# Attention and soft mixture-of-experts in one fp32 kernel: transposes in half-row pairs, one ring of four PSUM bank pairs, and one written-out order

## The chip, the cores and the metric

The kernel runs on one core of a Trainium2 chip. Its engines are TensorE (PE in the profile, with its weight loads shown apart as PEld), VectorE (DVE), ScalarE (ACT), GpSimd (POOL) and SyncE (SP), whose queue issues the DMAs. The metric is the device time of one execution in microseconds.

## The reference

Eight batches of eight heads attend over 576 positions of 64 values. The attention output, one row per token, goes through a soft mixture of experts: every token is spread over 32 slots (8 experts of 4), each expert is a two-layer network, and the slots are mixed back. All is fp32.

```python
scores = scale * q @ k.T + bias            # 576 x 576 per head; bias: a small MLP of positions
attn = exp(scores - max) / (sum + 1e-9)
x = (attn @ v)                             # heads side by side: 4608 tokens x 512
logits = x @ phi                           # 4608 x 32
d = softmax of logits over the tokens;  slot_input = d.T @ x
slot_out[e] = relu(slot_input[e] @ w1[e]) @ w2[e]
out = softmax of logits over the slots @ slot_out
```

## The kernel before

First the position bias of all heads is made (`bias_group`, 36 groups) and written to DRAM. Then come 32 units, `units`: four head pairs `hp`, each over eight batches. A unit has five row tiles p of queries. Row tiles 0 to 3 hold 128 queries of each of the two heads; row tile 4 holds the last 64 queries of both heads.

For each row tile, `score` (L257) multiplies queries with keys. The two heads stand in the lower and upper 64 rows of the PE array (L279), so the PE runs them as two 64x128 tiles; row tile 4 uses the whole array with a weight matrix that is half zeros (L270). DVE adds the bias and takes the extreme (L247), ACT takes the exponential and the sum (L250), DVE inverts the sum (L285, L286), and POOL scales the rows (L255). `turn` (L296) transposes the result 128x128 at a time (L309, L313, L317, L321), 41 blocks a unit, into single PSUM banks, which ACT or DVE copies to the tile `at` (`Split.copy`, L53 and L59, picks the engine by a running account). `mix` (L325) multiplies `at` with `v`: four parts with the two heads side by side in 64 columns each (L337), and a rest on the whole array (L340). The result `xt` goes to DRAM (`xs`) for the first three head pairs.

In the last head pair (units 24 to 31) `moe` (L346) does the token work of a batch beside the attention: it fetches the other heads' part back (`xo`, L353), transposes the tokens (L364, L370; 20 blocks), multiplies with `phi` (logits, L377), gathers running extremes and sums (L387, L389), transposes the powers (L431, L432) and sums into the slots (L463, L466). After unit 31 the experts' two layers run (L646, L673), with their weights `wt` streamed in, and the output is mixed and written (L702, L708).

Three PSUM pools hold the eight banks: `ps_s` two pairs, `ps_t` three single banks, `ps_o` one. The order of the attention comes from a loop over n = 5u + p: transposes run two row tiles behind the scores, and `mix` and the token steps are put in at offsets (`MIXL`, `MOEO`). The framework's scheduler then orders the instructions by its own estimate.

Of the kernel before, what the change touches and what calls it, by code (L numbers as in the profile page):

```python
# [19 lines left out]
W1N = 21  # L20
# [5 lines left out]
JB = (0, 0, 0, 0, 0)  # L26
MOEO = (1, 2, 2, 3, 3, 4, 5, 6, 6)
FEO = 0
FW = {(24, 2): 1, (31, 0): 1, (31, 1): 1, (31, 2): 1, (31, 3): 1, (31, 4): 1, (31, 8): 2, (31, 9): 3, 162: 1, 163: 1, 164: 3}
MIXE = (0.2, 0.2)  # L30
MOE1 = (1, 1, 2, 2, 2, 3, 5.3, 5.3, 5.8, 4, 5.8)
MOE2 = (0.7, 0.7, 0.7, 0.5, 0.7, 0.6, 0.9, 0.9, 0.95)
MIXL = ((2, 3), (1, 2))
# [31 lines left out]
def body(ctx, tc, qk, v, wcol, phi, mw1, mw2, tabh, consth, out):  # L65
# [23 lines left out]
    ld = Split(nc)  # L89

# [38 lines left out]
    def ready():  # L129

        nc.sync.dma_start(out=phis, in_=phi.rearrange("(g p) s -> p g s", p=P))
        with tc.issue_after(last["dve"].ins):
            nc.vector.tensor_scalar(out=phis, in0=phis, scalar1=-1.0, scalar2=None, op0=ALU.mult)
            nc.vector.tensor_add(out=rsum[:, 0:32], in0=ident[:, 0:32], in1=ident[:, 32:64])
            nc.vector.tensor_add(out=rsum[:, 0:32], in0=rsum[:, 0:32], in1=ident[:, 64:96])
            nc.vector.tensor_add(out=rsum[:, 0:32], in0=rsum[:, 0:32], in1=ident[:, 96:128])
            for r in range(1, 4):
                nc.vector.tensor_copy(out=rsum[:, 32 * r:32 * r + 32], in_=rsum[:, 0:32])
        with tc.issue_after(last["pool"].ins):
            for t in (lp, et, et2):  # L140
                nc.gpsimd.memset(t, 0.0)
# [11 lines left out]
    pc = ps_t.tile([P, 512], F32, name="pc", tag="t")  # L153
# [35 lines left out]
    def bias_group():  # L189
# [7 lines left out]
        pb = ps_s.tile([P, 2, 512], F32, name="pb", tag="s")  # L197
# [21 lines left out]
    def load_qk(u):  # L219


        hp, b = units[u]
        x = st[u]["qk"] = ldp.tile([P, 1280], F32, name="qk", tag="qk")
        nc.sync.dma_start(out=x, in_=qk[b, hp])
# [21 lines left out]
    def soft(ps, bias, y, mn, sm):  # L246
        last["dve"] = nc.vector.tensor_tensor_reduce(  # L247
            out=y.rearrange("a (x n) -> a x n", x=2), in0=ps[:, :, 0:HALF], in1=bias.rearrange("a (x n) -> a x n", x=2),
            scale=-QS, scalar=3.0e38, op0=ALU.add, op1=ALU.min, accum_out=mn)
        nc.scalar.activation(out=y, in_=y, func=AF.Exp, bias=mn, scale=-1.0, accum_out=sm)  # L250
        ld.a(851)
        ld.d(S)

    def norm(out, y, r):
        last["pool"] = nc.gpsimd.tensor_scalar(out=out, in0=y, scalar1=r, scalar2=1.0, op0=ALU.mult, op1=ALU.mult)  # L255

    def score(u, p):  # L257


        d = st[u]  # L260
        hp, b = units[u]
        x = d["qk"]
        y = d["y", p] = yp.tile([P, 2 * S], F32, name="y", tag="y")
        mn = smp.tile([P, 2], F32, name="mn", tag="mn")
        sm = smp.tile([P, 2], F32, name="sm", tag="sm")
        bias = biases[hp][p]
        if p == 4:
            ps = ps_s.tile([P, 2, 512], F32, name="ps", tag="s")
            for n in range(2):
                nc.tensor.matmul(ps[:, n, 0:HALF], x[:, 1152:1280], x[:, 64 + n * HALF:64 + (n + 1) * HALF], start=True,  # L270
                                 stop=True)
            soft(ps, bias, y[:, 0:S], mn[:, 0:1], sm[:, 0:1])
        else:
            pss = [ps_s.tile([P, 2, 512], F32, name="ps", tag="s") for _ in range(2)]
            for n in range(2):
                for hh in range(2):
                    rs = slice(64 * hh, 64 * hh + 64)
                    k0 = 64 * (1 - hh) + n * HALF
                    nc.tensor.matmul(pss[hh][:, n, 0:HALF], x[rs, 640 + p * P:640 + (p + 1) * P], x[rs, k0:k0 + HALF],  # L279
                                     start=True, stop=True, tile_position=(64 * hh, 0))  # L280
            for hh in range(2):
                hs = slice(S * hh, S * hh + S)
                soft(pss[hh], bias[:, hs], y[:, hs], mn[:, hh:hh + 1], sm[:, hh:hh + 1])
        r = sm[:, 0:1] if p == 4 else sm
        nc.vector.tensor_scalar(out=r, in0=r, scalar1=1e-9, scalar2=None, op0=ALU.add)  # L285
        nc.vector.reciprocal(out=r, in_=r)  # L286
        ld.d(0)
        ld.d(0)
        if p == 4:
            norm(y[:, S:S + 64], y[:, 512:576], r)  # L290
            norm(y[:, 0:S], y[:, 0:S], r)
        else:
            for g in range(2):
                norm(y[:, S * g:S * g + S], y[:, S * g:S * g + S], sm[:, g:g + 1])

    def turn(u, p, j):  # L296

        d = st[u]
        ch, cc = (p // 2, p % 2) if p < 4 else (1, 2)
        if p in (0, 2) and j == 0:  # L300
            d["at", ch] = atp.tile([P, 9, 256 + 64 * ch], F32, name="at", tag=f"at{ch}")
        at = d["at", ch]
        y = d["y", p]
        pt = ps_t.tile([P, 512], F32, name="pt", tag="t")
        if p < 4:
            if j < 2:
                for kk in range(4):
                    k0 = 640 * j + kk * P
                    nc.tensor.transpose(out=pt[:, kk * P:(kk + 1) * P], in_=y[:, k0:k0 + P], identity=ident)  # L309
                ld.copy(at[:, 4 * j:4 * j + 4, cc * P:(cc + 1) * P], pt.rearrange("a (x n) -> a x n", x=4), 512)  # L310
            else:
                for i in range(2):
                    nc.tensor.transpose(out=pt[:, i * P:(i + 1) * P], in_=d["y", p - 1 + i][:, 512:640], identity=ident)  # L313
                ld.copy(at[:, 8, 0:256], pt[:, 0:256], 256)
        elif j == 0:
            for kk in range(4):
                nc.tensor.transpose(out=pt[:, kk * P:(kk + 1) * P], in_=y[:, kk * P:(kk + 1) * P], identity=ident)  # L317
            ld.copy(at[:, 0:8, 256:320].rearrange("a (h k) n -> a k h n", h=2),
                    pt.rearrange("a (k h n) -> a k h n", k=4, h=2), 512)
        else:  # L320
            nc.tensor.transpose(out=pt[:, 0:P], in_=y[:, 512:640], identity=ident)  # L321
            ld.copy(at[0:64, 8, 256:320], pt[0:64, 0:64], 64)
            ld.copy(at[64:128, 8, 256:320], pt[64:128, 64:128], 64)

    def mix(u, ch, j):  # L325

        d = st[u]
        at, w = d["at", ch], 256 if ch == 0 else 320
        if j == 0:
            d["po", ch] = ps_o.tile([P, 512], F32, name="po", tag="o")  # L330
            if ch == 0:
                d["xt"] = xts[:, u % 2, :]
        po, xt = d["po", ch], d["xt"]
        for kk in (2 * j, 2 * j + 1):
            for hh in range(2):
                v0 = 64 * (4 * hh + kk)
                nc.tensor.matmul(po[64 * hh:64 * hh + 64, 0:w], d["v"][:, v0:v0 + 64], at[:, 4 * hh + kk, 0:w],  # L337
                                 start=kk == 0, stop=False, tile_position=(0, 64 * hh))
        if j == 1:
            nc.tensor.matmul(po[:, 0:w], d["v"][:, 512:640], at[:, 8, 0:w], start=False, stop=True)  # L340
            ld.copy(xt[:, 256 * ch:256 * ch + w], po[:, 0:w], w)
            hp, b = units[u]
            if ch == 1 and hp < NP - 1:
                nc.sync.dma_start(out=xs[b, hp], in_=xt)

    def moe(u):  # L346

        hp, b = units[u]
        m = {}

        def fetch():
            m["xo"] = xp.tile([P, NP - 1, S], F32, name="xo", tag="xo")
            nc.sync.dma_start(out=m["xo"], in_=xs[b].rearrange("g p j -> p g j"))  # L353

# [3 lines left out]
        def tokens(g):  # L358
            if g == 0:
                m["xk"] = xp.tile([P, 5, DM], F32, name="xk", tag="xk")  # L360
            gs = slice(g * P, (g + 1) * P)
            px = ps_t.tile([P, 512], F32, name="px", tag="t")
            for c in range(4):
                nc.tensor.transpose(out=px[:, c * P:(c + 1) * P], in_=X(g)[:, c * P:(c + 1) * P], identity=ident)  # L364
# [16 lines left out]
        def dispatch():  # L381
# [12 lines left out]
            for i, cs in parts:  # L394
                nc.vector.tensor_reduce(out=mb[:, i:i + 1], in_=pr[:, cs], axis=AX.X, op=ALU.min)
# [374 lines left out]
```

## Time and profile before

| | |
|---|---|
| time, median of 3 runs | 741.37 us (740.66 to 743.53) |
| the profiled execution's own time | 743.72 us |
| its span | 741.9 us |
| granted TensorE clock, mean | 0.989 |
| PE / DVE / ACT / POOL busy | 713.3 / 505.7 / 440.6 / 279.7 us |
| DMA moved | 111.52 MB |

The page gives busy time by engine, the span in 40 slices, the DMA queues and the costliest groups of instructions. A matmul's recorded duration includes its way through the array, so matmuls that follow each other overlap in the records: how fast the PE works is read from the distance between starts. In a timeline row the columns are start, duration of the merged group, engine, line, operation, tiles, shape and count. An fp32 matmul is two instructions, a transpose one.

### The profile page before, as it was taken

The numbers are of one execution on the slowest core, as the hardware profiler recorded it, in microseconds if no ns is written. First come the engines' busy times: TensorE is split into PE (matmuls) and PEld (weight loads), VectorE is DVE, ScalarE is ACT, GpSimd is POOL, SyncE is SP. The second block draws the span as 40 slices with busy tenths as digits, with TensorE's granted clock in tenths as the row PEclk, the third lists the DMA queues.
The fourth block names the chain that finished last, engine by engine and source line by source line (L and its number), as shares of the span: only waits on it lengthen the run. The fifth ranks groups of instructions, "written<-read, shape, count | busy, mean of one in ns | idle before, by whom it ended". The sixth has DMA issues, their size and how long they took to land. (4 is left out here: it accounts for less than half of the span.)

```text
span 741.9 us, 14863 instructions
## 1 busy us (share of the span) xinstructions
PE 713.3 (96%) x5295; PEld 434.8 (59%) x5295; DVE 505.7 (68%) x1416; ACT 440.6 (59%) x1043; POOL 279.7 (38%) x355
## 2 busy tenths in 40 slices
PE   6999999999999999999999999999999999989973
PEld 3334566666666666666666666665566556553542
DVE  8998876676676777677676677666767676552333
ACT  5776656666666666666666666656555556532233
POOL 7993544443444434434444444333222322200000
PEclk9999999999999999999999999999999999999997
DMA  6567992332622223372322237230233024476999
GB/s 226 198 207 248 341 356 93 103 93 87 210 71 70 70 73 103 99 213 75 118 70 70 77 102 220 90 98 22 86 101 101 23 81 144 168 257 204 351 362 331
DMA packets 54680, 111.52 MB, mean 150 GB/s; under 512 B 7120, under 2 KB 24784, under 8 KB 54608
## 3 DMA queue, kind: packets, MB, share of 16 engines
q1 hardware_dynamic: 54608, 110.59, 45.6%
q8 instruction: 42, 0.69, 0.4%
q14 instruction: 30, 0.25, 0.1%
HBM read 83.44 MB, written 27.13 MB: 149 GB/s over the span
## 5 line engine op out<-in xcount | busy, mean ns | idle before, releaser
L255 POOL TENSOR_SCALAR y<-y,sm 128x576 f32<-128x576 f32 (+1 forms) x320 | 221.6, 703 | 357.3 <-DVE sm L286 107.4
L250 ACT ACTIVATE y<-y,mn 128x576 f32<-128x576 f32 x288 | 221.5, 770 | 179.0 <-DVE mn L247 177.6
L247 DVE CUSTOM_DVE_ANT_0 y<-ps,bm 128x576 f32<-128x576 f32 x256 | 184.2, 758 | 49.9 <-PE ps L279 41.4
L279 PE MATMUL ps<-qk 64*128 64x288 f32 x1024 | 172.6, 430 | 0.6 <-DVE mn L247 0.5
L337 PE MATMUL po<-at,v 128*64 128x320 f32 (+1 forms) x1024 | 152.2, 418 | 1.1 <-ACT at L53 1.1
L309 PEld LDWEIGHTS pt<-ident,y 128*128 128x128 f32 x1024 | 114.4, 141 | 41.7 <-POOL y L255 22.7
L309 PE MATMUL pt<-ident,y 128*128 128x128 f32 x1024 | 137.9, 277 | 0.3 <-ACT at L53 0.3
L59 DVE COPY at<-pt 128x512 f32<-128x512 f32 (+2 forms) x188 | 107.5, 577 | 36.8 <-PE pt L309 26.6
L53 ACT COPY at<-pt 128x512 f32<-128x512 f32 (+2 forms) x228 | 107.1, 486 | 33.9 <-PE pt L309 30.3
L279 PEld LDWEIGHTS ps<-qk 64*128 64x128 f32 x1024 | 98.0, 186 | 35.3 <-issue 19.2
L337 PEld LDWEIGHTS po<-at,v 128*64 128x64 f32 x1024 | 62.2, 136 | 68.5 <-issue 29.6
L200 PE MATMUL pb<-f,wbd 128*32 128x64 f32 (+1 forms) x576 | 62.6, 421 | 2.2 <-DVE f L183 1.8
L183 DVE TENSOR_SCALAR f<-tabs,scl,nb 128x576 f32<-128x576 f32 x96 | 62.4, 727 | 0.6 <-DMA tabs<-in_tab_dram 0.6
L285 DVE TENSOR_SCALAR sm<-sm 128x2 f32<-128x2 f32 (+1 forms) x160 | 26.2, 163 | 53.3 <-ACT y L250 50.8
L183 POOL TENSOR_SCALAR f<-tabs,scl,nb 128x576 f32<-128x576 f32 x19 | 55.3, 2919 | 5.9 <-DMA tabs<-in_tab_dram 3.7
L250 ACT ACTIVATION_READ_ACCUMULATOR y<-y,mn 128x1 f32 x288 | 53.8, 187 | 0.0
L340 PE MATMUL po<-at,v 128*128 128x320 f32 (+1 forms) x128 | 48.1, 458 | 0.0
L200 PEld LDWEIGHTS pb<-f,wbd 128*32 128x32 f32 x576 | 24.1, 110 | 40.6 <-DVE f L183 20.6
L270 PE MATMUL ps<-qk 128*128 128x288 f32 x128 | 36.5, 407 | 0.0
L204 ACT ACTIVATE e<-pb,bcon 128x576 f32<-128x576 f32 x36 | 26.5, 737 | 15.7 <-PE pb L200 7.0
L340 PEld LDWEIGHTS po<-at,v 128*128 128x128 f32 x128 | 19.0, 188 | 28.0 <-issue 27.5
L247 DVE CUSTOM_DVE_ANT_0 y<-ps,br 128x576 f32<-128x576 f32 x32 | 24.2, 758 | 15.0 <-PE ps L270 14.5
(161 smaller groups left out, 560.6 us busy)
## 6 DMA issues: line engine op xcount, KB each, us to landing
wt<-in_moe_w_dram SPq DMA_DIRECT2D x64, 512.0 KB, 7.3
qk<-in_qk_dram SPq DMA_DIRECT2D x32, 640.0 KB, 5.1
v<-in_v_dram SPq DMA_DIRECT2D x32, 320.0 KB, 3.0
bias_m<-e SPq DMA_DIRECT2D x32, 288.0 KB, 2.3
out_dram<-ob SPq DMA_DIRECT2D x16, 512.0 KB, 5.2
xs<-xts SPq DMA_DIRECT2D x24, 288.0 KB, 2.9
xo<-xs SPq DMA_DIRECT2D x8, 864.0 KB, 6.6
bm<-bias_m SPq DMA_DIRECT2D x16, 288.0 KB, 2.9
```

What stands on the lines that cost most here:

```text
L53: nc.scalar.copy(out=out, in_=in_)
L59: nc.vector.tensor_copy(out=out, in_=in_)
L183: eng.tensor_scalar(out=f, in0=tabs[:, s0:s0 + S], scalar1=scl[:, sc:sc + 1], scalar2=nb1[:, 0:1], op0=ALU.mult, op1=ALU.max)
L200: nc.tensor.matmul(pb[32 * t:32 * t + 32, n, 0:w], wbd, fb[t][:, 512 * n:512 * n + w], start=True, stop=True, tile_position=(0, 32 * t))
L247: last["dve"] = nc.vector.tensor_tensor_reduce(out=y.rearrange("a (x n) -> a x n", x=2), in0=ps[:, :, 0:HALF], in1=bias.rearrange("a (x n) ...
L250: nc.scalar.activation(out=y, in_=y, func=AF.Exp, bias=mn, scale=-1.0, accum_out=sm)
L255: last["pool"] = nc.gpsimd.tensor_scalar(out=out, in0=y, scalar1=r, scalar2=1.0, op0=ALU.mult, op1=ALU.mult)
L270: nc.tensor.matmul(ps[:, n, 0:HALF], x[:, 1152:1280], x[:, 64 + n * HALF:64 + (n + 1) * HALF], start=True, stop=True)
L279: nc.tensor.matmul(pss[hh][:, n, 0:HALF], x[rs, 640 + p * P:640 + (p + 1) * P], x[rs, k0:k0 + HALF], start=True, stop=True, tile_position= ...
L309: nc.tensor.transpose(out=pt[:, kk * P:(kk + 1) * P], in_=y[:, k0:k0 + P], identity=ident)
L337: nc.tensor.matmul(po[64 * hh:64 * hh + 64, 0:w], d["v"][:, v0:v0 + 64], at[:, 4 * hh + kk, 0:w], start=kk == 0, stop=False, tile_position ...
L340: nc.tensor.matmul(po[:, 0:w], d["v"][:, 512:640], at[:, 8, 0:w], start=False, stop=True)
```

## The change

Half-row transposes: a 128x128 block is turned by two matmuls in transpose mode, one on the lower and one on the upper 64 rows, each with 64 moving columns of the identity and its own PSUM bank (`half_turn`). PSUM becomes four pairs of banks, handed round in order of release (`Banks`); scores, transposes, mixes and token steps all draw from it. Row tile 4's scores run as two 64x64 tiles without zeros, and the rest of `mix` as two 64-column tiles. Every step of attention and token work (S scores, t bias add, e exponential, m sum, n scale, T and R transposes, c copies, M mix, x copy of the mix, K, L, D, C, W, Z the token steps) gets a fixed place and, for copies, a fixed engine from a table, `PLAIN` for units 0 to 23 and `LAST` for 24 to 31; a place unit is a fifth of a unit. DMA loads are tied to steps of the table. The steps are issued in sorted order, and the framework's scheduler leaves them so.

```diff
+PLAIN = {
+    "lq": (-3.918, 0), "S0": (0.000, 0), "t0.0": (0.681, 0), "t0.1": (1.219, 0), "e0.0": (1.221, 0),
...
-    ps_s = ctx.enter_context(tc.tile_pool(name="ps_s", bufs=2, space=PSUM))
-    ps_t = ctx.enter_context(tc.tile_pool(name="ps_t", bufs=3, space=PSUM))
-    ps_o = ctx.enter_context(tc.tile_pool(name="ps_o", bufs=1, space=PSUM))
+    psp = ctx.enter_context(tc.tile_pool(name="psp", bufs=1, space=PSUM))
...
+    idle = [0, 1, 2, 3]
+
+    class Banks:
+        def __init__(self, n=1):
+            self.k, self.n = idle.pop(0), n
+            self.t = ps(self.k)
+
+        def read(self):
+            self.n -= 1
+            if self.n == 0:
+                idle.append(self.k)
+            return self.t
+
+    def then(u, name, f):
+        last = units[u][0] == NP - 1
+        place, eng = (LAST if last else PLAIN)[name]
+        prog.append((5 * u + place + (SHIFT if last else 0), len(prog), lambda: f(eng)))
...
+    def half_turn(out, src, r):
+        rs = slice(64 * r, 64 * r + 64)
+        nc.tensor.matmul(out, src[rs], ident[rs, rs], is_transpose=True, start=True, stop=True, tile_position=(64 * r, 0))
...
+                    if p == 4:
+                        nc.tensor.matmul(pss[0].t[rs, n, 0:HALF], x[rs, 1152:1216], x[rs, 64 + n * HALF:64 + (n + 1) * HALF],
+                                         start=True, stop=True, tile_position=(64 * hh, 64 * hh))
...
+        def turn(_):
+            pt = d["T", p] = Banks(2 if p < 4 else 3)
+            y = d["y", p]
+            for kk in range(8 if p < 4 else 5):
+                k0 = P * kk + 128 * (kk // 4) if p < 4 else P * kk
+                for r in range(2):
+                    half_turn(pt.t[:, r, 64 * kk:64 * kk + 64], y[:, k0:k0 + P], r)
+
+        step(u, f"T{p}", turn)
...
+                for hh in range(2):
+                    v0 = 64 * (4 * hh + i) if i < 4 else 512 + 64 * hh
+                    nc.tensor.matmul(po[64 * hh:64 * hh + 64, 0:w], d["v"][:, v0:v0 + 64],
+                                     d["at", c][:, 4 * hh + i if i < 4 else 8, 0:w], start=i == 0, stop=i == 4,
+                                     tile_position=(0, 64 * hh))
+
+            step(u, f"M{c}.{i}", part)
...
+        if u + 2 < U:
+            then(u, "S4", lambda _, u=u: load_qk(u + 2))
+            then(u, "M1.4", lambda _, u=u: load_v(u + 2))
+        if hp >= 1 and u - B < W1N:
+            then(u, "S1", lambda _: fetch_w(1))
...
+    with tc.manual_schedule():
+        for _, _, f in sorted(prog, key=lambda x: x[:2]):
+            f()
```

How the PE's rows stand in a unit of the first three head pairs. Before, two thirds of a unit (19 rows make a whole one): ps is a score, pt a transpose, po a mix.

```order
L279 MATMUL ps<-qk 128x288 x4
L337 MATMUL po<-at,v 64x320 x4
L309 MATMUL pt<-ident,y 128x128 x8
L279 MATMUL ps<-qk 128x288 x4
L337 MATMUL po<-at,v 64x320 x4
L340 MATMUL po<-at,v 128x320
L309 MATMUL pt<-ident,y 128x128 x8
L313 MATMUL pt<-ident,y 128x128 x2
L270 MATMUL ps<-qk 128x288 x2
L309 MATMUL pt<-ident,y 128x128 x8
L279 MATMUL ps<-qk 128x288 x4
L337 MATMUL po<-at,v 64x256 x4
```

Now, a whole unit; all PSUM tiles are called ps, L316 is `half_turn`, L338 and L334 are scores (L334 is row tile 4), L441 a mix:

```order
L441 MATMUL ps<-at,v 64x320 x10
L316 MATMUL ps<-ident,y 128x64 x20
L338 MATMUL ps<-qk 128x288 x8
L316 MATMUL ps<-ident,y 128x64 x16
L441 MATMUL ps<-at,v 64x256 x10
L316 MATMUL ps<-ident,y 128x64 x26
L338 MATMUL ps<-qk 128x288 x4
L316 MATMUL ps<-ident,y 128x64 x4
L334 MATMUL ps<-qk 64x288 x4
L338 MATMUL ps<-qk 128x288 x4
L316 MATMUL ps<-ident,y 128x64 x16
```

The mixes moved together into two runs of ten, and scores and transposes stand next to each other, both on 64-row tiles.

SP's queue around the fetch of `xo` in the last head pair, before:

```order
L229 DMA v<-in_v_dram 128x640
L224 DMA qk<-in_qk_dram 128x1280
L353 DMA xo<-xs 128x3x576
L229 DMA v<-in_v_dram 128x640
L224 DMA qk<-in_qk_dram 128x1280
```

and now (L258 qk, L263 v, L725 a weight tile, L464 the fetch):

```order
L258 DMA qk<-in_qk_dram 128x1216
L263 DMA v<-in_v_dram 128x640
L725 DMA wt<-in_moe_w_dram 128x1024
L464 DMA xo<-xs 128x3x576
L258 DMA qk<-in_qk_dram 128x1216
```

The fetch of unit u now stands behind the load of v for unit u + 2, which refills the buffer that the last mix part, M1.4, of unit u reads. The PE's rows between that part and the logits of unit u are these, now (the 64x320 row is M1.4; L594 and L595 transpose the powers, L640 and L643 sum into the slots, L509 is the logits, which read `xo`):

```order
L441 MATMUL ps<-at,v 64x320 x2
L441 MATMUL ps<-at,v 64x256 x2
L594 MATMUL ps<-ident,et_93 128x128
L595 MATMUL ps<-ident,et_93 128x32
L441 MATMUL ps<-at,v 64x256 x2
L316 MATMUL ps<-ident,y 128x64 x20
L338 MATMUL ps<-qk 128x288 x4
L640 MATMUL ps<-xk,ek 32x512 x4
L643 MATMUL ps<-xk,ek 32x128 x4
L509 MATMUL ps<-xo,phis 32x288 x3
```

Before, the transposes of the `xo` tokens are what first reads a new `xo`, some 12 us after its issue, and the logits of the same batch come later.

More of the change, by code (lines that the diff above doesn't have):

```diff
@@ L260, in score, with rows, scores @@
+    def rows(u, p):
         d = st[u]
         hp, b = units[u]
[L262 to L274, printed above, removed]
+        c, cc = (p // 2, p % 2) if p < 4 else (1, 2)
+        heads = (0, 1) if p < 4 else (0,)
+        def scores(_):
+            x = d["qk"]
+            d["ps", p] = pss = [Banks() for _ in heads]
@@ L277, in score @@
                     rs = slice(64 * hh, 64 * hh + 64)
[L278 to L284, printed above, removed]
@@ L325, in mix @@
[L325 to L344, printed above, removed]
+                    if p == 4:
+                        nc.tensor.matmul(pss[0].t[rs, n, 0:HALF], x[rs, 1152:1216], x[rs, 64 + n * HALF:64 + (n + 1) * HALF],
+                                         start=True, stop=True, tile_position=(64 * hh, 64 * hh))
+                    else:
+                        k0 = 64 * (1 - hh) + n * HALF
+                        nc.tensor.matmul(pss[hh].t[:, n, 0:HALF], x[rs, 640 + p * P:640 + (p + 1) * P], x[rs, k0:k0 + HALF],
+                                         start=True, stop=True, tile_position=(64 * hh, 0))
@@ new lines, in mix, with part, keep @@
+    def mix(u, c):
+        d = st[u]
+        hp, b = units[u]
+        w = 256 + 64 * c
+        for i in range(5):
+            def part(_, i=i):
+                if i == 0:
+                    d["po", c] = Banks()
+                po = d["po", c].t[:, 0]
+                for hh in range(2):
[4 more added lines that the diff above has]
+            step(u, f"M{c}.{i}", part)
+        def keep(eng):
+            d["xt"] = xts[:, u % 2, :]
+            cp(eng, d["xt"][:, 256 * c:256 * c + w], d["po", c].read()[:, 0, 0:w])
+            if c == 1 and hp < NP - 1:
+                nc.sync.dma_start(out=xs[b, hp], in_=d["xt"])
+        step(u, f"x{c}", keep)
@@ L475, in slots @@
[L475 removed]
                 return
[L477 to L479 removed]
+            for cc in range(5):
+                rs = slice(0, P if cc < 4 else 64)
                 for g in range(4):
[L481 to L482 removed]
@@ L641, in body @@
     for Q in range(2):
[L642 removed]
+        ph = ps(Q)
         for kc in range(4):
```

523 lines of the change are left out of this document (277 added, 246 removed), and 32 rows, old and new, of tables (LAST, PLAIN).

## The prediction

> **What bounds the kernel now.** I read the page first: busy time, slices, then the stages.
>
> ```profile
> span 741.9 us, 14863 instructions
> PE 713.3 (96%) x5295; PEld 434.8 (59%) x5295; DVE 505.7 (68%) x1416; ACT 440.6 (59%) x1043; POOL 279.7 (38%) x355
> PE   6999999999999999999999999999999999989973
> PEclk9999999999999999999999999999999999999997
> DMA  6567992332622223372322237230233024476999
> ```
>
> PE is busy in every slice but the edges, at full clock. DMA fills only the start and the end. The stages (columns after the window's length: PE, PEld, DVE, ACT, POOL, clock, DMA share, GB/s) say the same:
>
> ```profile
> 200.00:300.00 100.00, 100.00 (x690) 66.08 (x690) 71.15 (x214) 64.45 (x160) 41.67 (x61) 1.00 0.28 85
> 542.30:566.70 24.40, 24.35 (x182) 14.53 (x181) 17.25 (x52) 14.59 (x41) 7.02 (x12) 1.00 0.25 78
> 680.00:742.00 62.00, 43.58 (x441) 25.90 (x438) 22.30 (x43) 19.54 (x38) 0.00 (x0) 0.92 0.93 318
> ```
>
> From about 70 to 640 us PE sets the pace; from 680 us on the DMA does (share 0.93). A busy PE is not yet a PE at its peak, so the third view is PE's timeline over one unit:
>
> ```profile
> 302.82 0.27 PE L321 MATMUL pt<-ident,y 128*128 128x128 f32 x1
> 303.02 1.24 PE L279 MATMUL ps<-qk 64*128 64x288 f32 x8
> 304.19 1.30 PE L337 MATMUL po<-at,v 128*64 128x320 f32 x8
> 305.42 1.09 PE L309 MATMUL pt<-ident,y 128*128 128x128 f32 x8
> 306.44 1.24 PE L279 MATMUL ps<-qk 64*128 64x288 f32 x8
> ...
> 309.48 1.04 PE L309 MATMUL pt<-ident,y 128*128 128x128 f32 x8
> 310.35 0.38 PE L313 MATMUL pt<-ident,y 128*128 128x128 f32 x2
> 310.57 1.14 PE L270 MATMUL ps<-qk 128*128 128x288 f32 x4
> ...
> 319.46 1.24 PE L279 MATMUL ps<-qk 64*128 64x288 f32 x8
> ```
>
> A unit lasts 319.46 - 303.02 = 16.44 us. Eight transposes behind work of their own shape take 310.35 - 309.48 = 0.87 us: 0.109 each for 128 columns, 0.85 ns a column. At that rate a unit streams: scores 5 x 4 x 288 columns = 4.91 us, mixes 10 x (256 + 320) = 4.91, transposes 41 x 128 = 4.47; together 14.29. (An fp32 matmul passes twice; two tiles side by side pass at once.) The other 2.15 us sit where the array's tile shape changes: the first score group takes 304.19 - 303.02 = 1.17 us for 0.98 of streaming, the transposes behind a mix 306.44 - 305.42 = 1.02 for 0.87. A unit changes shape twelve times (64x128, 128x64, 128x128 in turn), 0.18 us each.
>
> **The change: transposes.** A block now streams 64 columns instead of 128, 0.054 us, if both halves run at once; but each half still loads weights of 128 columns. What such a load costs when nothing covers it, five small transposes show, whose 32 columns stream in 0.027 us:
>
> ```profile
> 663.10 0.49 PE L435 MATMUL pe<-ident,et 32*128 32x32 f32 x5 [0.37 <-ACT et L422]
> 663.10 0.38 PEld L435 LDWEIGHTS pe<-ident,et 32*128 32x128 f32 x5 [0.64 <-ACT et L422]
> L435 PEld LDWEIGHTS pe<-ident,et x5: 134/137/138, 663.1 to 663.3; 32*128 32x128 f32 x5
> ```
>
> The loads start (0.38 - 0.137) / 4 = 0.061 us apart. Whether the loads of two row halves run side by side, the scores tell, which are such a pair:
>
> ```profile
> L279 PEld LDWEIGHTS ps<-qk 64*128 64x128 f32 x1024 | 98.0, 186 | 35.3 <-issue 19.2 <-DVE mn L247 2.1 <-DVE xts L59 1.8
> ```
>
> 1024 loads of 186 ns are 190 us of load in 98.0 us of busy time: two at a time. So I take 0.062 us a block, nearest to L435. The floor is 0.054; the ceiling is 0.124, two loads one after the other. A unit's 41 blocks fall from 4.47 to 2.54 us.
>
> **Shape changes.** Scores and transposes now share the 64x128 shape, the rest of the mix shares the mixes' shape, and the zeros of row tile 4 become two 64x64 tiles that stream the same 288 columns. By the order there are six changes a unit: into and out of each of two mix runs and of row tile 4. 6 x 0.18 = 1.08 us instead of 2.15. A unit's sum is 4.91 + 4.91 + 2.54 + 1.08 = 13.44 us.
>
> **Waits in the new order.** What evacuates PSUM must keep up:
>
> ```profile
> L247 DVE CUSTOM_DVE_ANT_0 y<-ps,bm 128x576 f32<-128x576 f32 x256 | 184.2, 758 | 49.9 <-PE ps L279 41.4 <-DMA bias_r<-e 2.5 <-POOL y L255 1.4
> L59 DVE COPY at<-pt 128x512 f32<-128x512 f32 x136 | 93.4, 687 | 32.6 <-PE pt L309 26.6 <-PE pt L317 5.9
> L53 ACT COPY at<-pt 128x512 f32<-128x512 f32 x152 | 86.8, 576 | 31.2 <-PE pt L309 30.3 <-PE pt L317 0.5
> ...
> 304.40 0.76 DVE L247 CUSTOM_DVE_ANT_0 y<-ps,bm 128x576 f32<-128x576 f32 x1 [0.41 <-PE ps L279]
> 305.08 0.75 DVE L247 CUSTOM_DVE_ANT_0 y<-ps,bm 128x576 f32<-128x576 f32 x1
> ```
>
> DVE's share of 71% in a unit of 16.44 us is 11.7 us, ACT's 64% is 10.6. The copies stay as many and as large (nine of 512 a unit; DVE now has 4, before 136 / 32 = 4.25), so in 13.9 us DVE is at 84% and ACT at 76%: neither becomes the bound on its sum. The ring: a pair of banks is held while it fills, some 0.3 us until its reader starts, and while it is read. From the rows that is about 2.05 us for a score that DVE reads first, 2.7 for the second of the two, 1.4 for a transpose, 0.8 for a rest, 3 for a mix: 36 us for a unit's 18 fillings, 36 / 4 = 9.0 us over four pairs. Below 13.9, so the ring binds only in places: T3 stands behind two score pairs and needs the bank of the first bias add, the mix run after it that of the second, 0.68 us later (304.40 to 305.08). I charge 0.45 us a unit for such hand-overs, an estimate between 0 and the 1.7 of the rival below. The unit comes to 13.9 us, 2.54 less than now; units 0 to 23 give 24 x 2.54 = **61 us**.
>
> **Other queues.** POOL's 42% becomes 50%; its scalings have about a unit until the transposes read them. On SP the loads hang on steps of the table now:
>
> ```profile
> qk<-in_qk_dram SPq DMA_DIRECT2D x32, 640.0 KB, 5.1
> v<-in_v_dram SPq DMA_DIRECT2D x32, 320.0 KB, 3.0
> ```
>
> qk for unit u + 2 is issued after S4 of unit u and read 5.2 places later, v after M1.4 and read 6.5 places later: 14 and 18 us at 2.78 us a place, against 5.1 and 3.0 to land. The bias loads of the next head pair go out over its last unit, one unit ahead of their readers. These cost nothing; if a store of `xs` in front of them held SP up, there are 9 us to spare.
>
> **Units 24 to 31.** These last 24.41 us:
>
> ```profile
> 542.26 1.14 PE L270 MATMUL ps<-qk 128*128 128x288 f32 x4
> ...
> 566.67 1.14 PE L270 MATMUL ps<-qk 128*128 128x288 f32 x4
> ```
>
> Of this 41 x 0.047 = 1.93 us go with the attention's blocks, 20 x 0.047 = 0.94 with the tokens'. The order counts 29 changes of shape in such a unit before and 19 now: 10 x 0.18 = 1.8. That is 4.67 us. Against it stand 0.45 of hand-overs, 0.5 for the transposes of the powers, which now follow closely on the exponentials that they read (an estimate), and a new wait. It is in the other order of SP's queue:
>
> ```profile
> 544.55 0.38 SPq L353 DMA_DIRECT2D xo<-xs  x1
> DMA to landing us min/median/max: 6.0/6.6/7.1
> ...
> 552.50 0.33 PE L431 MATMUL pe<-ident,et 128*128 128x128 f32 x1
> 552.94 1.08 PE L337 MATMUL po<-at,v 128*64 128x256 f32 x8
> ...
> 556.73 0.55 PE L364 MATMUL px<-ident,xo 128*128 128x128 f32 x3
> 557.33 1.06 PE L463 MATMUL pd<-xk,ek 128*32 128x512 f32 x8
> 558.33 0.42 PE L466 MATMUL pd<-xk,ek 64*32 64x128 f32 x8
> 558.68 0.33 PE L364 MATMUL px<-ident,xo 128*128 128x128 f32 x1
> ```
>
> Before, `xo` is issued at 544.55 and first read at 556.73: 12.2 us for a landing of 6.0 to 7.1. Now it queues behind the v load that waits for M1.4, and a weight tile: two issues of 0.33 us and a landing of 6.6 put it 7.3 us behind M1.4. In that time PE has two mix parts (0.44), the powers' transposes (552.94 - 552.50 = 0.44), ten blocks (0.62), a score group (0.98), the slots (558.68 - 557.33 = 1.35), four changes (0.7, part of them in the figures) and the 0.5 above: about 4.8. Then the logits wait 2.5 us, and behind them in PE's queue the token transposes, two transposes and a score group, so that DVE and ACT run dry too. Net a unit gains 4.67 - 0.95 - 2.5 = 1.2; eight give 10 us. For the last two the fetch has weight tiles ahead of it, two or more of 512 KB: 2 us more each, an estimate. Left: **6 us**.
>
> **Start and end.** The bias groups are unchanged, and load and store sizes almost so. The end waits for DMA (0.93, 318 GB/s) in the old sequence of tiles, hidden from PE's gain: zero, between -10 (weights asked for earlier) and +5 (single buffers for the last copies).
>
> **The sum.** 61 + 6 = 67 us off the profiled execution's 743.72 (span 741.9) gives 676.7. The three runs' median, 741.37, is 2.35 below that execution, so the forecast in the metric is 741.37 - 67 = **674 us**.
>
> **Rivals.**
> *Halves one after the other (slower).* If the two loads of a block, or the issue of its four instructions, do not overlap, a block costs 0.124 us. 32 x 41 + 8 x 20 = 1472 blocks at 0.062 more: +91, **765 us**. It decides from 67 / 1472 = 0.045 above my price, a block of 0.107. For it: L435's ten instructions took 0.31 us, the pace of 0.124 for four. Against it: the score loads run two at a time. Chance 0.09.
> *Loads at the plain rate.* L340's first load in a mix costs more than a transpose's:
>
> ```profile
> 308.84 0.81 PE L340 MATMUL po<-at,v 128*128 128x320 f32 x2
> L340 PE MATMUL po<-at,v 128*128 128x320 f32 x64 | 25.8, 485 | 0.0
> ```
>
> Its two starts are about 0.81 - 0.43 = 0.38 us apart (0.43 is its second record; the mean of 485 holds both) for 0.27 of streaming: 0.107 for 128 columns. At that price a block saves nothing: +1472 x 0.045 = 66, **740 us**. L435's 0.061 at the same 128 columns speaks against it. Chance 0.06.
> The Trainium skill (TensorE: Matmul & The Clock Gate, LDWEIGHTS) has this as its rule: a load's time goes by columns, not rows, at 1.2 a nanosecond, so 64 rows load as slowly as 128. By it 128 columns are 107 ns and this rival is the forecast; L340 agrees, L435 in transpose mode does not.
> *No wait for xo.* If the fetch lands in time, 8 x 2.5 + 4 = 24 us come back: **650 us**. Chance 0.20.
> *Evacuation.* If every bank's reader stands behind two bias adds (2 x 0.68 us), the mean hold grows from 2.0 to 3.36 us, and 18 x 3.36 / 4 = 15.1 us is the unit, 1.2 more: +39, **713 us**. DVE at 84% with a strict order speaks for it, the sum of 9.0 us against. Chance 0.19.
> The Trainium skill (TensorEngine Tiling (Array Packing), PSUM Bottleneck) warns of this: tiling speeds up the array and not the evacuation, which may become the bottleneck. No row here shows it at four pairs.
>
> **How the numbers follow.** The forecast, with hand-overs of 0 to 0.9 us a unit (660 to 690), has 0.46. The range goes from 640, below the case without the xo wait with a few microseconds from the end, to 722, above the evacuation case; it leaves out the two load rivals (0.15) and the far edges. A measurement tells 0.5%, 3.7 us, from no change. Faster by more: 0.46 + 0.20 + 0.19 = 0.85. Within: 0.06, the plain-rate case. Slower: 0.09.
>
> **What would show it.** Right: about 13.9 us from one row-tile-4 score to the next in units 0 to 23; blocks 0.062 us apart; six shape changes; PE's logits row in units 24 to 31 with idle time ended by the DMA of `xo`, near 2.5 us. Wrong: blocks at 0.107 or 0.124; PE idle before scores or transposes ended by DVE or ACT for more than a microsecond a unit; an end longer than now.

## The result, and the profile after

The changed kernel takes 731.9 us (median of 4 runs, 728.51 to 732.85) against 741.82 us on the same chip, a ratio of 0.986 (0.982 to 0.990). The prediction was 674, range 640 to 722: the direction was right, but about 85% of the gain of 67 us did not come. The page of the profiled execution (731.29 us, span 729.5), in its rows for PE, the granted clock and DMA:

```profile
span 729.5 us, 18273 instructions
PE 641.0 (88%) x7023; PEld 389.5 (53%) x7023; DVE 473.2 (65%) x1367; ACT 471.8 (65%) x1076; POOL 279.1 (38%) x355
PE   6999689999999999999999997968978998679883
PEclk9999989999999999999999999888999999769997
DMA  6556212233733343644433482213212344646998
```

PE's busy time fell from 713.3 to 641.0 us, but the span by 12.4 only. The work went; idle time took its place. In PE's row (slices counted from 0) there is a gap at slices 4 and 5, where the attention begins; the others begin at slice 24, about 445 us, where units 24 to 31 begin, and the clock falls with them. The starts of the row-tile-4 scores cut the span into stages:

| stage | before | after | difference | predicted |
|---|---|---|---|---|
| start, to unit 0's row-tile-4 score | 78.3 | 80.3 | +2.0 | 0 |
| from unit 0's to unit 24's | 396.7 | 365.1 | -31.6 | -61 |
| from unit 24's to unit 31's | 166.8 | 160.8 | -6.0 | -6, with the next row |
| from there to the first feed-forward matmul | 26.2 | 48.2 | +22.0 | |
| from there to the end | 73.9 | 75.1 | +1.2 | 0 |

In the first 24 units PE's timeline shows a period and a wait:

```profile
293.49 1.19 PE L334 MATMUL ps<-qk 64*64 64x288 f32 x8 [0.77 <-ACT at L284]
...
305.33 1.03 PE L316 MATMUL ps<-ident,y 64*128 64x64 f32 x26
306.19 1.19 PE L338 MATMUL ps<-qk 64*128 64x288 f32 x8
307.21 0.29 PE L316 MATMUL ps<-ident,y 64*128 64x64 f32 x4
308.27 1.19 PE L334 MATMUL ps<-qk 64*64 64x288 f32 x8 [0.77 <-ACT at L284]
```

The unit is 308.27 - 293.49 = 14.78 us; 13.9 was predicted. Each unit PE waits 0.77 us for a ScalarE copy (L284) before the row-tile-4 scores (L334). The transposes are as fast as predicted: the 26 half-row instructions last 1.03 us to the end of the last, whose own record is about 0.23 long, so their starts are (1.03 - 0.23) / 25 = 0.032 us apart, 0.064 a block against 0.062. Of the whole execution's waits these rows bear on the prediction (us in total, times, longest):

```profile
ACT at L284 <- DVE at L284: 57.1, 63, 3.6
DVE xk L284 <- ACT xk L284: 42.8, 14, 7.7
PE ps L509 <- DMA xo<-xs: 21.4, 7, 5.4
PE ps L334 <- ACT at L284: 20.2, 25, 1.3
```

The first two are copies that wait for copies. The strip of a transpose lies in a bank pair, and ScalarE's copy of one bank waits for VectorE's copy of the other. The two read different banks and write different columns; what they share is the tile that they read, and the program lets the second wait for the first. That the shared tile is the reason is argued, not tested alone, but the other traces fit it: in the kernel before and in experiment 4 each bank is a tile of its own, both engines write the same `at`, and no copy of `at` or `xk` waits for a copy; in experiment 3, with pair tiles and whole transposes, ScalarE's copies wait for VectorE's 63 times again (66.7 us). The second row is mostly the late fetch's: in experiment 1 it is 17.3 us. The third is the predicted wait for `xo`, longer than predicted. What such a wait leaves behind is seen in PE's timeline near the end:

```profile
617.73 0.42 PE L643 MATMUL ps<-xk,ek 64*32 64x128 f32 x8
623.00 0.70 PE L509 MATMUL ps<-xo,phis 128*32 128x288 f32 x3 [4.84 <-DMA xo<-xs]
623.02 0.69 PE L509 MATMUL ps<-xts,phis 128*32 128x288 f32 x1
623.45 0.73 PE L509 MATMUL ps<-xo,phis 128*32 128x288 f32 x3
```

After 4.84 us without work the logits start 0.45 to 0.48 us apart. Where no wait stands before them it is 0.24 to 0.27 (from the timeline of experiment 1, below):

```profile
596.63 0.44 PE L509 MATMUL ps<-xo,phis 128*32 128x288 f32 x3
...
596.90 0.42 PE L509 MATMUL ps<-xo,phis 128*32 128x288 f32 x3
...
597.14 0.42 PE L509 MATMUL ps<-xo,phis 128*32 128x288 f32 x3
```

So they ran at half the clock: the granted clock is 0.50 from 623 to 625 us, and 1.00 in the rows of experiment 1. The Trainium skill (TensorE: Matmul & The Clock Gate, Part 1) says that an idle window of about 3.4 us halves the clock; this row agrees. Between units 0 and 1 the clock falls too, where no single wait of PE's is as long (2.22 us at most; under "The seams" below).

### The profile page after: what moved, and what is told of

It reads as the page before. It is cut to its first block, busy times and chain, and to the rows that moved or that the text cites. A ratio compares the mean times of both kernels' runs of the same rounds, so it can differ in the third digit from the quotient of the medians.

```text
span 729.5 us, 18273 instructions
## 1 busy us (share of the span) xinstructions
PE 641.0 (88%) x7023; PEld 389.5 (53%) x7023; DVE 473.2 (65%) x1367; ACT 471.8 (65%) x1076; POOL 279.1 (38%) x355
## 5 line engine op out<-in xcount | busy, mean ns | idle before, releaser
L441 PE MATMUL ps<-at,v 128*64 128x256 f32 (+1 forms) x1280 | 174.6, 416 | 0.7 <-ACT at L284 0.7
L338 PE MATMUL ps<-qk 64*128 64x288 f32 x1024 | 171.0, 431 | 1.1 <-ACT at L284 0.9
L284 ACT COPY at<-ps 128x512 f32<-128x512 f32 (+2 forms) x264 | 126.9, 501 | 65.6 <-DVE at L284 57.1
L316 PEld LDWEIGHTS ps<-ident,y 64*128 64x128 f32 x2624 | 109.4, 143 | 51.0 <-POOL y L281 18.3
L316 PE MATMUL ps<-ident,y 64*128 64x64 f32 x2624 | 124.6, 231 | 10.8 <-POOL y L281 6.3
L338 PEld LDWEIGHTS ps<-qk 64*128 64x128 f32 x1024 | 105.1, 192 | 40.3 <-DVE mn L351 10.7
L441 PEld LDWEIGHTS ps<-at,v 128*64 128x64 f32 x1280 | 85.8, 138 | 57.6 <-DVE mn L351 2.9
L284 DVE COPY at<-ps 128x512 f32<-128x512 f32 (+2 forms) x152 | 82.8, 557 | 40.0 <-PE ps L316 27.0
L234 PE MATMUL ps<-f,wbd 128*32 128x64 f32 (+1 forms) x576 | 63.1, 420 | 3.1 <-DVE f L217 2.7
L334 PE MATMUL ps<-qk 64*64 64x288 f32 x256 | 38.2, 416 | 21.0 <-ACT at L284 20.2
L234 PEld LDWEIGHTS ps<-f,wbd 128*32 128x32 f32 x576 | 23.7, 110 | 41.9 <-issue 21.5
L284 DVE COPY xk<-ps 128x512 f32<-128x512 f32 x16 | 11.0, 690 | 42.8 <-ACT xk L284 42.8
L238 ACT ACTIVATE e<-ps,bcon 128x576 f32<-128x576 f32 x36 | 26.5, 737 | 16.4 <-ACT f L213 6.5
L509 PE MATMUL ps<-xo,phis 128*32 128x288 f32 x96 | 14.2, 582 | 22.7 <-DMA xo<-xs 21.4
```

The costliest lines, as they stand in the source:

```text
L234: nc.tensor.matmul(pb[32 * t:32 * t + 32, n, 0:w], wbd, fb[t][:, 512 * n:512 * n + w], start=True, stop=True, tile_position=(0, 32 * t))
L238: nc.scalar.activation(out=e, in_=pb.rearrange("a x n -> a (x n)")[:, 0:S], func=AF.Identity, bias=bc)
L284: (nc.vector.tensor_copy if eng else nc.scalar.copy)(out=out, in_=in_)
L316: nc.tensor.matmul(out, src[rs], ident[rs, rs], is_transpose=True, start=True, stop=True, tile_position=(64 * r, 0))
L334: nc.tensor.matmul(pss[0].t[rs, n, 0:HALF], x[rs, 1152:1216], x[rs, 64 + n * HALF:64 + (n + 1) * HALF], start=True, stop=True, tile_positi ...
L338: nc.tensor.matmul(pss[hh].t[:, n, 0:HALF], x[rs, 640 + p * P:640 + (p + 1) * P], x[rs, k0:k0 + HALF], start=True, stop=True, tile_positio ...
```

## The experiments

All times are medians; the ratio is to the kernel before, measured on the same chip.

**1. The fetch of `xo` earlier.**

```diff
-    "fx": (12.840, 0),
+    "fx": (10.500, 0),
```

> The changed kernel with one number altered: the fetch of the token tile xo stands at 10.500 instead of 12.840 in the order of units 24 to 31, behind the token transposes of the unit before and ahead of the next v load. Theory A (the 21.4 us that the logits wait for xo, 7 times, are the landing time of a transfer that is issued just ahead of its reader): the seven waits fall below 3 us in all, and PE's clock, 0.90 in the stretch from unit 24 to the feed-forward matmuls, rises; 731.9 becomes 700 to 712. Rival B (the wait only stands in front of others, for POOL's scaled rows, the copies and the serial token chain at the end): the waits for xo go, others grow by as much, and the time is 722 to 731.

Measured: 700.58 us, ratio 0.943 (0.940 to 0.945). Theory A, at the edge of its range. PE's waits no longer hold a row for `xo`, and the others did not grow (6.3 us for POOL's rows in the change too, and 5.5 for `ob`):

```profile
PE ps L334 <- ACT at L284: 20.2, 25, 1.3
PE ps L316 <- POOL y L281: 6.3, 6, 3.0
PE ps L852 <- ACT ob L87: 5.2, 5, 1.7
```

The period of units 26 to 31 is 20.66 us (before the change 24.41), and from unit 24's row-tile-4 score to the feed-forward it is 178.9 us: 193.0 before, 209.0 with the late fetch. One number in the table was worth 31 us, of which 21.4 stood in the trace as waits for the DMA (and 2.5 more of PEld's). The rest is what they dragged along: the same instructions kept PE busy longer at the lower clock. From unit 24's row-tile-4 score to the feed-forward they took 171.1 us in the change and 130.5 + 33.1 = 163.6 here, 7.5 less (change first; columns: start and end, length, busy time of PE, PEld, DVE, ACT and POOL, clock, DMA share, GB/s; the 33.1 stand in a row of experiment 4):

```profile
445.40:654.40 209.00, 171.11 (x1969) 104.26 (x1969) 115.27 (x379) 126.75 (x319) 53.20 (x83) 0.90 0.34 115
```

```profile
445.00:584.80 139.80, 130.52 (x1602) 82.00 (x1602) 92.79 (x301) 105.51 (x265) 49.10 (x76) 0.98 0.33 110
```

**2. One copy for a strip instead of two.**

```diff
-            for r in range(2):
-                def keep(eng, r=r):
-                    n0 = cc * P + 64 * r
-                    cp(eng, target()[:, 0:8, n0:n0 + 64], d["T", p].read()[:, r].rearrange("a (x n) -> a x n", x=8))
+            def keep(eng):
+                cp(eng, target()[:, 0:8, cc * P:cc * P + P].rearrange("a x (r n) -> a r x n", r=2),
+                   d["T", p].read().rearrange("a r (x n) -> a r x n", x=8))
```

> The changed kernel with the two copies of a transposed strip (one PSUM bank each, on VectorE and on ScalarE) made one copy of both banks: strips 0 and 3 on ScalarE, 1 and 2 on VectorE in units 0 to 23, all on ScalarE after that. Theory A (the second copy of a pair waits for the first although each reads its own bank, and the row-tile-4 scores wait for the second): VectorE 0.685 and then ScalarE 0.568 us become one copy of about 0.96 (an estimate from 0.568 us at 512 columns and 0.371 at 256), so the wait ahead of these scores falls from 0.77-0.97 us to about 0.5, the unit from 14.78 to about 14.4, and the time to 718 to 724. Rival B (the scores' wait comes from the place of the copies in their engines' order, behind the adds and the exponentials, not from the pair): the wait stays at 0.8 to 1.0 and the time at 730 to 734. Rival C (longer single copies hold other banks and block the engine behind them): new waits ahead of other transposes, 735 to 745.

Measured: 730.89 us, ratio 0.981 (0.976 to 0.987), no difference from the change that can be told. The unit stayed at 14.79 us, and its timeline says why:

```profile
292.52 1.19 PE L334 MATMUL ps<-qk 64*64 64x288 f32 x8 [0.33 <-ACT at L284]
...
298.82 1.78 PE L338 MATMUL ps<-qk 64*128 64x288 f32 x8
300.82 1.24 PE L338 MATMUL ps<-qk 64*128 64x288 f32 x8 [0.23 <-DVE at L284]
```

The wait that theory A spoke of fell from 0.77 to 0.33 us, but the scores of row tile 1 stretched from 1.24 to 1.78 us and those of row tile 2 began to wait: they need the bank pair that VectorE now empties in one copy of 1.21 us. Theory A holds for the wait and rival C for what took its place, though C's time (735 to 745) did not come; the time lies in rival B's range, but by B the wait would have stayed at 0.8 to 1.0. That the unit came out the same made it doubtful that copies bound it; experiments 5 and 6 were made to test that.

**3. The order alone, with whole transposes.** The table, the ring and the row-tile-4 scores stay; a block is again one 128x128 transpose, blocks 0 to 3 of a strip in one bank, the rest in the other.

```diff
-                for r in range(2):
-                    half_turn(pt.t[:, r, 64 * kk:64 * kk + 64], y[:, k0:k0 + P], r)
+                nc.tensor.transpose(out=pt.t[:, kk // 4, P * (kk % 4):P * (kk % 4) + P], in_=y[:, k0:k0 + P], identity=ident)
```

> The changed kernel's order and ring, with whole 128x128 transposes in place of the half-row ones everywhere. Theory A (the half-row blocks are worth 0.045 us each, 41 a unit, and the order itself is worth nothing or costs): the unit goes from 14.78 to between 15.9 and 16.7 (a part of the 1.85 us falls into the wait ahead of the row-tile-4 scores), the time to 760 to 785. Rival B (the order brought the gain): the unit stays within 0.5 us of 14.8 and the time at 731 to 745.

Measured: 776.40 us, ratio 1.046 (1.044 to 1.048). Theory A: the unit is 16.55 us, where it was 16.44 before and is 14.78 with half rows. The order alone is slower than the kernel before. Before the row-tile-4 scores, here L337, three waits are left, 1.9 us in all, presumably because the longer transposes cover the copies; no run tests that.

**4. The half rows alone, in the order of before.**

```diff
+            if j == 0:
+                pt2 = ps_t.tile([P, 512], F32, name="pt", tag="t")
+                for kk in range(8):
+                    k0 = kk * P + 128 * (kk // 4)
+                    for r, o in ((0, pt), (1, pt2)):
+                        rs = slice(64 * r, 64 * r + 64)
+                        nc.tensor.matmul(o[:, 64 * kk:64 * kk + 64], y[rs, k0:k0 + P], ident[rs, rs], is_transpose=True,
+                                         start=True, stop=True, tile_position=(64 * r, 0))
...
+                    ld.copy(at[:, 0:8, n0:n0 + 64], o.rearrange("a (x n) -> a x n", x=8), 512)
```

> The kernel before with half-row transposes for the strips of row tiles 0 to 3 alone: both halves at once into its two single-bank transpose tiles, each tile copied by the planner's choice of engine; order, queues, the transposes of the remaining columns, of row tile 4 and of the tokens unchanged. 32 blocks a unit at 0.064 instead of 0.109 us are 1.44 us a unit. Theory A (PE bounds that order too, and two separate tiles are copied side by side): the unit goes from 16.44 to 15.0 to 15.8, the time to 700 to 722. Rival B (both tiles have to be free at once, so each strip waits for both copies of the strip ahead): new waits of PE on the copies, 735 to 760.

Measured: 715.61 us, ratio 0.964 (0.962 to 0.965). Theory A; the unit is 15.66 us. This small part of the change beats the whole. The stretch that grew by 22 us in the whole change, from the last row-tile-4 score to the feed-forward, comes with the order. That stretch in this kernel, in experiment 3, in the change and in experiment 1, in this turn (columns as in experiment 1):

```profile
613.20:639.10 25.90, 22.57 (x226) 13.20 (x224) 14.96 (x49) 9.93 (x28) 2.53 (x4) 1.00 0.81 272
```

```profile
650.30:701.90 51.60, 39.59 (x306) 22.70 (x305) 22.48 (x78) 19.67 (x54) 4.12 (x7) 0.81 0.48 165
```

```profile
606.20:654.40 48.20, 35.46 (x369) 18.98 (x369) 22.50 (x78) 20.18 (x55) 4.12 (x7) 0.83 0.53 181
```

```profile
584.80:623.80 39.00, 33.07 (x368) 17.82 (x368) 22.42 (x78) 20.03 (x55) 4.12 (x7) 0.91 0.66 224
```

With the old order 22.6 us of PE work and 49 VectorE instructions are left there, with the new one 78 and, even with the early fetch, 33.1 us of PE.

**5. The small copy that stands in VectorE's way.**

```diff
-    "cr4.0": (9.417, 1),
+    "cr4.0": (9.417, 0),
```

> The changed kernel with one engine altered in units 0 to 23: the small copy of row tile 4's upper half (cr4.0, 64x64) goes to ScalarE, behind the two copies of the same bank pair that ScalarE makes already, instead of to VectorE, where it waits for them while the next unit's first strip copy (c0.0) is queued behind it. Theory A (the wait of 0.77 us ahead of the row-tile-4 scores is a chain of copies that wait for each other: c4 and cr4.1 on ScalarE, cr4.0 on VectorE, c0.0 on VectorE, c0.1 on ScalarE): c0.0 starts some 0.5 us earlier, the wait falls to 0.2 to 0.4, the unit from 14.78 to 14.2 to 14.4, the time from 731 to 718 to 723. Rival B (something else holds the unit at 14.78, as the run with one copy a strip might suggest, where the wait moved and the unit stayed): the wait turns up ahead of another group of matmuls and the time stays at 728 to 733.

Measured: 726.28 us (720.66 to 729.60), ratio 0.979 (0.974 to 0.984). The unit is 14.32 us with 0.31 of wait, theory A's figures. From unit 0 to unit 24 it took 13.5 us less, 3.0 of them in the first step of unit to unit, which the theory says nothing of. The time missed its range: in this execution units 24 to 31 took 6.2 us more, with 24.1 us of waits for `xo` in place of 21.4. While that wait is there, its length varies and hides gains elsewhere.

**6. One ScalarE copy for strip 0 alone.**

```diff
-"c0.0": (4.522, 1), "c0.1": (4.683, 0),
+"c0": (4.522, 0),
```

> The changed kernel with a single ScalarE copy of both banks for strip 0 alone, in units 0 to 23; strips 1 to 3 keep their two copies. In the run with one copy for every strip the wait ahead of the row-tile-4 scores fell from 0.77 to 0.33 us, but the scores of row tile 1 took 1.78 instead of 1.24 us behind a VectorE copy of 1.21 us. Theory A: without those long VectorE copies only the first half of that remains, the unit is 14.3 to 14.4 and the time 718 to 723. Rival B (the unit is held at 14.78 by something else): 728 to 733.

Measured: 718.81 us (716.75 to 721.64), ratio 0.970 (0.967 to 0.973): theory A, unit 14.30 us. With experiment 5 this shows that the chain of copies in front of the row-tile-4 scores held the unit for some 0.5 us: it was shortened in two different ways.

**7. Experiments 1 and 5 together.**

> The early fetch of xo (700.6 alone) and the small copy on ScalarE together. Theory A (the two losses lie in different units, 24 to 31 and 0 to 23, and add up): 700.6 less 9 to 13 us, 687 to 692. Rival B (the unit of the first 24 is held by something else): 697 to 701.

Measured: 689.59 us, ratio 0.929 (0.927 to 0.931). The two losses add up.

**8. The same with the two tables closer together.**

```diff
-SHIFT = 2.0
+SHIFT = 0.5
```

> The same two edits with the shift of the places of units 24 to 31 against those of units 0 to 23 at 0.5 instead of 2.0. Theory A (the step from unit 23 to 24, 18.57 us where a unit takes 14.78, is lost at the seam between the two tables because the shift holds back the next unit's steps): 2 to 4 us below the run without it, 684 to 688. Rival B (the shift is what keeps the steps of both tables apart; without it units 23 and 24 get in each other's way): 0 to 5 us above that run.

Measured: 691.99 us, ratio 0.933 (0.930 to 0.936). Rival B: the step from unit 23 to 24 grew from 18.68 to 20.89 us.

**9. A kernel that takes all this together.** Experiments 1 and 6, and `cr4.1` on VectorE beside `cr4.0`.

> The early fetch of xo, one ScalarE copy for strip 0 in units 0 to 23, and in these units both small copies of row tile 4 (cr4.0, cr4.1) on VectorE, so that ScalarE goes straight from c4 to strip 0. Theory A (the 0.3 us that were left ahead of the row-tile-4 scores are ScalarE's small copy, 0.2 us, and the rest of the chain): wait 0 to 0.1 us, unit 14.0 to 14.1 (the 14.01 us of PE work that the changed kernel's unit holds without its wait), time 689.6 less 5 to 7 us, 682 to 685. Rival B (VectorE's two small copies delay its adds, and PE waits there instead): unit 14.3 to 14.6, 688 to 695.

Measured: 680.68 us (679.76 to 684.94), ratio 0.917 (0.915 to 0.918), the fastest of all and a little below theory A's range. The unit is 14.03 us, theory A's figure, with no wait reported before these scores:

```profile
294.37 0.29 PE L316 MATMUL ps<-ident,y 64*128 64x64 f32 x4
294.68 1.19 PE L335 MATMUL ps<-qk 64*64 64x288 f32 x8
...
308.70 1.19 PE L335 MATMUL ps<-qk 64*64 64x288 f32 x8
```

**10. The state's merge later.**

```diff
-    "d3": (17.165, 0),
+    "d3": (18.240, 0),
```

> The same, and the state update of the tokens' softmax (d3, with the three small matmuls that merge the two halves of the state, 2.3 us of waits one behind the other after unit 31's scores) goes behind the slots of unit 30 and the logits and first token transposes of unit 31. Theory A (the 39 us between unit 31's last scores and the feed-forward matmuls, 26.2 before the change, are work that the deeper order has left for the end, with waits of some 6 us in all): 0.5 to 2 us less. Rival B (these waits are what makes the end long, through the clock that falls behind them): 4 to 8 us less.

Measured: 685.00 us (680.12 to 689.21), ratio 0.923 (0.920 to 0.926), slower than experiment 9: neither theory. The merge's waits moved next to the fold that reads its result (rows of this kernel):

```profile
590.24 0.58 PE L694 MATMUL ps<-stS,rsum 128*128 128x1 f32 x2 [0.78 <-DVE stS L693]
592.47 0.66 PE L701 MATMUL ps<-acc,rsum 128*32 128x128 f32 x8 [1.65 <-DVE acc L698]
```

The stretch before the feed-forward is 44.1 us here, 39.9 in experiment 9. The two traced executions took 680.12 us here and 684.94 in experiment 9, the other way round than the medians: the first step of unit to unit, to which this edit does nothing, is 15.96 us here and 19.55 there.

## Why the prediction was right and wrong

**Blocks: right.** 0.064 us against 0.062. In the new order half rows were worth 16.55 - 14.78 = 1.77 us a unit, though 0.77 of wait came up with them; 1.93 was the term. The rivals of one half after the other (0.124) and of the plain load rate (0.107) are out. The rule of the Trainium skill (TensorE: Matmul & The Clock Gate, LDWEIGHTS), by which 128 columns take 107 ns whatever the rows, does not hold for these loads in transpose mode.

**Hand-overs: the step that failed in the first 24 units.** I charged 0.45 us "between 0 and the 1.7 of the rival below", from how long a bank is held. Measured were 0.77 before the row-tile-4 scores, and about 0.7 more in a place where PE's rows report no wait (next paragraph): some 1.4 us. The sum without hand-overs, 13.44, falls short of the unit, 14.78, by 1.34. The sum of holds was a mean, and the place I named (T3, behind two bias adds) was not it. What I left out is a dependence of one copy on another: I took a pair's two copies for parallel, one on each engine, as they were before. The evacuation rival (15.1 us a unit) came nearest to the unit, but by another mechanism: its readers stood behind bias adds. Experiments 5, 6 and 9 took the wait from 0.77 to 0.31, 0.29 and nothing in PE's rows, and the unit from 14.78 to 14.32, 14.30 and 14.03. The Trainium skill (TensorEngine Tiling (Array Packing), PSUM Bottleneck) advises to empty PSUM with both ScalarE and VectorE; here it paid to give strip 0's pair to ScalarE alone (experiment 6); with every strip in one copy, two of them on VectorE, the unit gained nothing (experiment 2).

**Shape changes: right, with a second hand-over beside them.** Experiment 9's unit has no wait in PE's rows and is 14.03 us, 0.6 above the 13.44. Blocks at 0.064 instead of 0.062 add 0.08. The rest lies in one place of experiment 9's timeline:

```profile
296.87 0.66 PE L316 MATMUL ps<-ident,y 64*128 64x64 f32 x16
297.45 2.91 PE L449 MATMUL ps<-at,v 128*64 128x320 f32 x20
...
300.97 2.56 PE L339 MATMUL ps<-qk 64*128 64x288 f32 x15
303.14 0.37 PE L316 MATMUL ps<-ident,y 64*128 64x64 f32 x3
303.37 0.40 PE L339 MATMUL ps<-qk 64*128 64x288 f32 x1
303.38 0.89 PE L316 MATMUL ps<-ident,y 64*128 64x64 f32 x13
304.20 2.38 PE L449 MATMUL ps<-at,v 128*64 128x256 f32 x20
```

The scores of row tiles 1 and 2 (sixteen instructions) and a strip, up to the next mix, take 304.20 - 300.97 = 3.23 us. The scores stream for 1.96, and a strip up to the next mix takes 297.45 - 296.87 = 0.58 in the other place: 0.69 are too many. The rows of the weight loads show why, first in this place, then in all from 100 to 410 us, some 22 units, with ScalarE's waits below them:

```profile
302.54 0.54 PEld L339 LDWEIGHTS ps<-qk 64*128 64x128 f32 x5 [0.35 <-ACT at L284]
```

```profile
PEld ps L339 <- ACT at L284: 7.8, 22, 0.4
```

```profile
ACT at L284 <- DVE at L284: 17.1, 22, 0.8
```

A copy that waits for a copy again: the loads of row tile 2's scores wait 0.35 us in every unit for ScalarE's copy of strip 2, and that copy waits 0.8 for VectorE's copy of the other bank. By the order of issue it is the second head's bank pair that is missing. The first head's matmuls go on without it, so PE is not idle and its rows report nothing, but the two heads no longer run side by side, and the last score is left among the transposes (303.37). The change has the same wait (7.4 us in 21 times). No run was made to remove it; that it costs the whole 0.69 is read from these rows. It leaves 14.03 - 0.69 - 4.91 - 4.91 - 41 x 0.064 = 0.90 us for the six changes of shape, for which 1.08 was the term.

**The seams: not in the sum.** I took 24 x 2.54. The first step of unit to unit was 20.84 us (18.53 before) and the one into unit 24 18.58 (16.44 before), so two of the 24 steps lost 2 us each in place of gaining 2.5: 9.5 us. The first varies with the clock: experiments 9 and 10 have the same table for these units, and it is 19.55 us in one and 15.96 in the other. The granted clock is 0.80 there in experiment 9 (78 to 99 us), and the row-tile-4 scores take 80.85 - 78.74 = 2.11 us and a run of mixes 95.78 - 92.21 = 3.57; in experiment 10 the clock is 1.00, and they take 1.12 and 2.31. In the change it is 0.76 (80 to 101 us). No single wait of PE's is longer than 2.22 us there in any of the three. Experiment 8 shows that less distance between the tables makes the second longer, not shorter; what it consists of is open.

**The wait for `xo`: right mechanism, wrong size.** 2.5 us a unit was the term and 24 us the price in all; there were seven waits of 3 us on average, and removing them brought 31. The step missed the clock: I priced a wait by its length alone, and 7.5 us of the 31 are matmuls that ran slower behind the waits.

**The end of the attention: not in the sum.** For units 24 to 31 I took the gain of a unit eight times. With the early fetch the period is 20.66 us, 3.75 below 24.41, as 4.67 - 0.95 = 3.72 says; the terms of that sum were not measured one by one. But from the last row-tile-4 score to the feed-forward it is 39.0 us instead of 26.2 even then: the deeper order leaves more to be done when no later unit covers it, 12.8 us here. Experiments 3 and 4 show that this comes with the order; no run has a shallower one. "Start and end: zero" looked at loads and stores and not at what the pipeline still holds when the units run out.

**Account.** The span was to fall by 67 us and fell by 12.4; 54.6 are missing. The other 22 steps up to unit 24 took 325.7 us, 14.80 on average, and hold 22 x (14.80 - 13.90) = 19.9 of it (two of them are some 0.2 us longer than the 14.78), the two seams 9.5, the stretch from unit 24's scores to the feed-forward 16 + 6 = 22 (6 for what the fetch cost beyond the 24 us, which is 209.0 - 178.9 = 30.1 in this stretch, 13 for the end of the attention, 3 not placed), and start and end 3.2. Experiment 9 takes 680.7 us, which is near the forecast of 674 by luck: the forecast held 24 us for a late fetch that experiment 9 does not have, and nothing for the seams and the end of the attention, which it has.

## What to carry to other kernels

When two buffers are made into one, look for what was parallel because they were two: each reader's wait in the new program has to be read, not only its sum of time. Read the waits of the weight loads too: where two tiles share the array, one that waits does not make PE idle. A transfer that lands just after its reader costs its wait and, if the wait is long, the clock behind it, so issue it as soon as its buffer is free. A deeper order is paid for once at each end, and that belongs into the sum.

## What the runs showed of the hardware

Two half-row transposes on the two halves of the array really run side by side: 0.064 us for both, 0.109 for the whole block. After 4.84 us without work PE ran the logits at half pace (0.45 to 0.48 us between starts), at a granted clock of 0.50; the whole stretch before the feed-forward had 0.83, against 0.91 with the fetch moved and 1.00 in experiment 4. Between units 0 and 1, where no wait of PE's is longer than 2.22 us, the granted clock was 0.80 in experiment 9 and 1.00 in experiment 10, on the same steps. In experiment 2 a ScalarE copy of two banks took 1.01 us on average where one of a single bank took 0.57, and VectorE's 1.21 where one of a single bank takes 0.68 in the change: one long copy saves 11 to 12%.
